# Fused attention and gated MLP: one scaling step of the 64-bit weights on GpSimd instead of ScalarE, with a new order list

## The chip, the cores and the metric

The kernel runs on one core of a Trainium2 chip. A core has five engines that run side by side, each with a queue of its own: TensorE (PE; its weight loads are shown as PEld), VectorE (DVE), ScalarE (ACT), GpSimd (POOL) and SyncE (SP), which here only issues transfers. The metric is the device time of one execution in microseconds, the median of several runs.

## The reference, cut to what matters

```python
# attention, per batch (8) and head (8); seq = 576, head_dim = 64
scores = scale * np.matmul(q, k.transpose(0, 1, 3, 2))
mask = (rel >= 0) & (rel < 128)
scores = np.where(mask, scores + bias[None], -1000000000.0)
attn = softmax(scores)                      # max subtracted, sum + 1e-9
x = matmul(attn, v), heads side by side     # 8 x 576 x 512
# gated MLP on x
h = gelu_tanh(x @ w_in)                     # w_in 512 x 1024
u, v = h[..., :512], h[..., 512:]
v_n = (v - mean) / sqrt(var + 1e-06) * g_ln
v_s = einsum('ts,bsd->btd', w_sg, v_n) + b_sg
out = x + (u * v_s) @ w_out                 # w_out 512 x 512
```

`w_in` and `w_out` come as 64-bit floating point numbers. Each is loaded as pairs of 32-bit words and turned into a high and a low 32-bit part on the chip, and every product with them is three products (high by high, high by low, low by high).

## The kernel before, in words

The work is cut into small named steps. `add` registers a step with its engine, a length and the steps it comes after; the text `ORDER` lists all of them, and they are emitted in exactly that order, so that each engine's queue is the list cut down to that engine's steps. A step waits only for what it reads or overwrites, but nothing on an engine passes the step ahead of it.

There are 32 pairs of heads, four to a batch. For a pair with number n the steps are: `q` and `L` load queries with keys, and values (SP). `a` and `c`, or `*` for both from pair 5 on, are the score products (TensorE). `A B C G` shift and mask the scores and take their minima (VectorE; L305 and L298). `e E f F j` are the exponentials with their sums (ScalarE, L314). `R` inverts the sums (VectorE, L325 and L326; it needs all five exponentials). `r`, `s` (ScalarE for the first four pairs, L332, GpSimd after) and `S` (GpSimd, L337) scale. `z`, `t` and `T` transpose (TensorE, L363 and L350). `P` copies and `X` and `Y` mask the transposes (ScalarE; VectorE, L359). `V` is the product with the values (TensorE, L387). `p` and `x` (ScalarE) and `2` (VectorE, L399) collect it. `h` (ScalarE, L404) and `l` (GpSimd, L221) make its high and low part for the MLP, and `k` copies a tail. In the list the step of the kind `2` for pair 0 reads `20`.

The weights come in twelve blocks k of 128 rows by 512 columns: 0 to 7 for `w_in`, 8 to 11 for `w_out`. Each runs through this chain: `i` loads it (SP, L182) into one of four buffers, which is free again behind `+`. `d` has two ScalarE instructions: L193 scales the low words by 2^-29 in place, from unsigned to signed integers, and L195 takes the absolute value of the high word as a float. `m`, `b` and `o` (VectorE, L197, L199 and L201) clamp, shift and join the bits. `+` (GpSimd, L221) adds the scaled low words, an integer add over all 512 columns. `H` (ScalarE, L206) rounds to the high part, and `-` (VectorE L211 for odd k, GpSimd for even) leaves the low part. `wl`, `wH`, `w-` do the same for the matrix `w_sg`, and `tl`, `tH`, `t-`, `bl`, `bH`, `b-` for its tail and the bias; they share the four buffers. A load that finds none free waits, and the loads behind it on SP's queue wait with it.

The MLP of the first batch begins while the pairs 4 and 5 are in work: `w` followed by two digits and `v0` are the products of the value half (L609 to L611, the first digit is the block of rows, the second the pair), `vg` their gelu (ScalarE, L788; it needs a table load when the last function was an exponential), `nv` and `vn` the normalization, `u` the products of the other half, `uc` their copies (ScalarE, L842), `y` the gate products and `gm` the gating. `W` are idle products on zeros (TensorE, L1141), 51 in twelve steps.

From about 63 us on TensorE does one product behind the other; the later batches use the same steps with fewer products. The part of the list that changes ends in the first fifth of the time.

Of the kernel before, what the change touches and what calls it, by code (L numbers as in the profile page):

```python
# [21 lines left out]
def attention_gmlp(  # L22
# [1125 lines left out]
    for b in range(B):  # L1148
# [14 lines left out]
        r4 S4 w-0 t4 25 X4 nt0b nt0p u010 z4 T4 u011 Y4 nt0c P4 uc02 d11 bH V4 nt0h p4 x4 uc01 ug0 b- tn0 m11 m8 24  # L1163
        b11 o11 b8 y000 y001 *7 +11 gm00 A7 o8 +8 B7 C7 j7 e7 H11 -11 Us0 y020 y021 y030 G7 gm02 Us1 E7 H8 -8 gh00 f7
        h4 gh02 F7 Us2 *6 y010 Us3 R7 A6 B6 C6 s7 t7 S7 T7 y031 E6 gl02 r7 gl00 G6 X7 f6 e6 j6 F6 z7 y011 h5 L7 L6 q8
        q9 Y7 R6 gm03 gm01 P7 V7 gh03 gh01 p7 Uh0 s6 r6 S6 gl01 t6 T6 X6 x7 27 Y6 Oa0 gl03 z6 O00 P6 V6 Us4 oa00 h7
        Uh1 x6 p6 l7 l4 l5 26 Ul0 Ul1 O01 *8 A8 B8 C8 Us5 G8 h6 k5 f8 j8 e8 l6 u100 u101 k6 k7 E8 *9 Us6 F8 oa01 Us7
# [105 lines left out]
```

## Time and profile before

| | us |
|---|---|
| median of 3 runs | 581.13 (581.12 to 581.57) |
| the profiled execution | 581.97 |
| its span, first to last instruction | 580.3 |
| TensorE busy | 563.5 (97%) |
| VectorE busy | 476.9 (82%) |
| ScalarE busy | 381.4 (66%) |
| GpSimd busy | 309.1 (53%) |

The span lies 1.67 us inside the time of its own execution, and that execution 0.84 us above the median. Busy shares over the whole span say little here, since the first 63 us and the rest have different limits; the rows of the next section are read by stretches.

### The profile page before, as it was taken

How to read it: one execution, taken by the hardware profiler on the slowest of the kernel's cores; microseconds unless marked ns; L12 is line 12 of the kernel's file. 1: busy time of each engine (PE TensorE's matmuls, PEld its weight loads, DVE VectorE, ACT ScalarE, POOL GpSimd, SP SyncE). 2: the span in 40 equal slices, each digit the busy share in tenths (PEclk: the TensorE clock that was granted, in tenths of full speed). 3: DMA queues.
4: the chain of work that ended last, by engine and by line, in shares of the span. 5: the costliest groups of instructions: out<-in, count | busy, mean ns of one | idle time of the engine just before them, and what ended most of it. 6: DMA issues, size and time to landing. Idle time of an engine off the chain costs nothing.

```text
span 580.3 us, 14668 instructions
## 1 busy us (share of the span) xinstructions
PE 563.5 (97%) x5495; PEld 514.3 (89%) x5495; DVE 476.9 (82%) x1336; ACT 381.4 (66%) x1066; POOL 309.1 (53%) x365
## 2 busy tenths in 40 slices
PE   6898899999999999999999999999999999999997
PEld 5676799999899799998999998998999989998997
DVE  8998999789989878899787987878897988666646
ACT  7899997375754776568776585746695666833422
POOL 4657645730335643664447753486447653476325
PEclk9979999999999999999999999999999999999999
DMA  8773332080602613454250365135432606012502
GB/s 299 212 224 107 127 102 83 7 272 33 210 37 64 215 37 98 144 180 141 60 184 38 105 236 167 48 101 153 143 121 64 211 4 196 3 32 98 171 1 82
DMA packets 43562, 69.79 MB, mean 120 GB/s; under 512 B 3554, under 2 KB 31202, under 8 KB 43492
## 3 DMA queue, kind: packets, MB, share of 16 engines
q1 hardware_dynamic: 43492, 68.86, 36.8%
q8 instruction: 43, 0.70, 0.5%
q14 instruction: 27, 0.22, 0.1%
HBM read 56.27 MB, written 12.58 MB: 119 GB/s over the span
## 4 chain that ended last, share of the span: by engine, by line
PE 86%; DVE 4%; DMA 3%; ACT 3%; POOL 2%; issue 1%; SPq 0%; DVEq 0%; POOLq 0%
PE ps_m L1061 13%; PE ps_m L609 12%; PE ps_m L907 12%; PE ps_m L611 11%; PE ps_m L610 11%; PE ps_a L350 4%; PE ps_a L281 4%; PE ps_s L387 3%; PE ps_m L387 3%; PE ps_s L281 3%; DMA wst<-w_sgT 2%; DMA qk<-qkT 1%; PE ps_m L943 1%; PE ps_m L942 1%; DVE e L298 1%
## 5 line engine op out<-in xcount | busy, mean ns | idle before, releaser
L337 POOL TENSOR_TENSOR e<-e,rr 128x256 f32<-128x256 f32 (+2 forms) x116 | 80.3, 715 | 95.1 <-DVE rr L326 90.5
L314 ACT ACTIVATE e<-e,stats 128x128 f32<-128x128 f32 (+1 forms) x288 | 110.6, 386 | 19.4 <-DVE stats L298 18.9
L227 POOL TENSOR_TENSOR region<-u,region 128x288 fp32r<-128x288 f32 (+1 forms) x78 | 77.6, 1014 | 44.8 <-ACT region L1008 16.2
L359 DVE TENSOR_TENSOR px<-ps_a,m_both 128x1024 f32<-128x1024 f32 x64 | 77.4, 1215 | 6.2 <-PE ps_a L350 4.9
L609 PE MATMUL ps_m<-ws,region 128*128 128x288 f32 x256 | 78.3, 306 | 0.0
L611 PE MATMUL ps_m<-ws,region 128*128 128x288 f32 x256 | 75.7, 296 | 0.0
L610 PE MATMUL ps_m<-ws,region 128*128 128x288 f32 x256 | 75.6, 295 | 0.0
L732 POOL TENSOR_TENSOR rs<-rs,mhalf 128x1 f32<-128x1 f32 (+1 forms) x40 | 30.6, 766 | 58.3 <-DVE rs L729 54.6
L221 POOL TENSOR_TENSOR xs<-xf,xs 128x288 fp32r<-128x288 f32 (+1 forms) x48 | 51.1, 1086 | 14.5 <-ACT xs L404 14.5
L314 ACT ACTIVATION_READ_ACCUMULATOR e<-e,stats 128x1 f32 x288 | 54.3, 189 | 0.0
L1008 ACT ACTIVATE region<-u 128x576 fp32r<-128x576 f32 x35 | 23.6, 684 | 43.4 <-PE ps_m L610 17.4
L609 PEld LDWEIGHTS ps_m<-ws,region 128*128 128x128 f32 x256 | 48.3, 189 | 1.5 <-issue 1.1
L610 PEld LDWEIGHTS ps_m<-ws,region 128*128 128x128 f32 x256 | 48.2, 188 | 0.1
L611 PEld LDWEIGHTS ps_m<-ws,region 128*128 128x128 f32 x256 | 48.1, 188 | 0.1
L609 PE MATMUL ps_m<-wi,xs 128*128 128x512 f32 x112 | 46.7, 417 | 0.9 <-ACT vg L788 0.9
L1068 DVE TENSOR_TENSOR xf<-ps_m,xf 128x576 f32<-128x576 f32 x48 | 35.7, 750 | 10.9 <-PE ps_m L1061 10.1
L611 PE MATMUL ps_m<-wi,xs 128*128 128x512 f32 x112 | 44.3, 395 | 0.0
L610 PE MATMUL ps_m<-wi,xs 128*128 128x512 f32 x112 | 44.2, 395 | 0.0
L948 DVE TENSOR_TENSOR u<-ps_m,u 128x576 f32<-128x576 f32 x32 | 24.0, 750 | 19.7 <-PE ps_m L943 12.6
L350 PE MATMUL ps_a<-ident,e 128*128 128x128 f32 x256 | 38.0, 276 | 0.2
L298 DVE CUSTOM_DVE_ANT_0 e<-ps_s,bias 128x128 f32<-128x128 f32 (+1 forms) x140 | 34.9, 286 | 2.6
L1061 PE MATMUL ps_m<-region,sum 128*128 128x288 f32 x252 | 36.5, 298 | 0.0
(213 smaller groups left out, 1606.2 us busy)
## 6 DMA issues: line engine op xcount, KB each, us to landing
qk<-qkT SPq DMA_DIRECT2D x32, 576.0 KB, 4.5
sum<-store SPq DMA_DIRECT2D x36, 512.0 KB, 5.0
...
```

The lines of the kernel that those rows point to most:

```text
L221: (engine or nc.gpsimd).tensor_tensor(out[:, cs], a[:, cs], b[:, cs], op)
L227: nc.gpsimd.tensor_tensor(out[:, fs], a[:, fs], b[:, fs], ALU.subtract)
L298: nc.vector.tensor_tensor_reduce(out=dst, in0=src, in1=bs, scale=-1.0 / math.sqrt(D), scalar=3e38, op0=ALU.add, op1=ALU.min, accum_out=acc)
L314: nc.scalar.activation(x, x, AF.Exp, bias=self.nm[0:n, i:i + 1], scale=-1.0, accum_out=self.sm[0:n, i:i + 1])
L337: nc.gpsimd.tensor_tensor(x[:, z:z + step, :], y[:, z:z + step, :], self.rr[0:n, i + z:i + z + min(k, step)].rearrange("p (m o) -> p m o", ...
L350: burst([lambda t=t: nc.tensor.transpose(cv[:, t // 2, t % 2], self.pr[j][:, t, :].rearrange("p (h c) -> p h c", h=2), ident[:, j * R:j * ...
L359: nc.vector.tensor_tensor(xv, cv, mv, ALU.mult)
L609: nc.tensor.matmul(dst, ah, bh, start=(first and i == 0), stop=False)
L610: nc.tensor.matmul(dst, ah, bl, start=False, stop=False)
L611: nc.tensor.matmul(dst, al, bh, start=False, stop=(last and i == n - 1))
L907: nc.tensor.matmul(dst, left(n, g, c)[:, ms], right(n, h, c), start=first and c == 0 and k == 0, stop=c == 1 and k == 2, skip_group_check= ...
L1061: nc.tensor.matmul(dst, p, q, start=first and f == 0 and k == 0, stop=f == 1 and k == 2, skip_group_check=True)
```

## The change

The scaling of the low words leaves the step `d` and becomes a step of its own, `n`, on GpSimd (`third`, twelve times). `d` keeps only the absolute value. `+` now comes after both `o` and `n`. The list is new up to `u101`, the second batch's last product of that kind in the changed part; behind it nothing moves. Only the first lines of the two lists are shown, as far as the text follows them.

```diff
--- before.py
+++ after.py
@@ -182,6 +182,11 @@
         nc.sync.dma_start(w[0:src.shape[0]], src)
         return w
 
+    def third(w):
+
+        w0 = w.bitcast(U32).rearrange("p (n t) -> p n t", t=2)[:, :, 0]
+        nc.gpsimd.tensor_scalar(w0.bitcast(I32), w0, 2.0 ** -29, None, ALU.mult)
+
     def split64(hi, lo, w, f, last):
 
 
@@ -189,8 +194,6 @@
         w1 = w.bitcast(I32).rearrange("p (n t) -> p n t", t=2)[:, :, 1]
         w1f = w.bitcast(F32).rearrange("p (n t) -> p n t", t=2)[:, :, 1]
         fi, ri = f.bitcast(I32), w0.bitcast(I32)
-
-        nc.scalar.activation(ri, w0, AF.Copy, scale=2.0 ** -29)
 
         nc.scalar.activation(f, w1f, AF.Abs)
         yield
@@ -545,11 +548,12 @@
             next(got["steps"])
 
         add(f"i{k}", "SP", 1.55, at - 8.0, load, take=[("g", [f"+{k}"])], lag=2.0)
-        add(f"d{k}", "ACT", 1.13, at, begin, [f"i{k}"], take=take_f)
+        add(f"d{k}", "ACT", 0.57, at, begin, [f"i{k}"], take=take_f)
+        add(f"n{k}", "POOL", 0.65, at, lambda: third(got["w"]), [f"i{k}"])
         add(f"m{k}", "DVE", 0.34, at, go, [f"d{k}"], port=True)
         add(f"b{k}", "DVE", 0.43, at, go, [f"m{k}"], port=True)
         add(f"o{k}", "DVE", 0.61, at, go, [f"b{k}"], port=True)
-        add(f"+{k}", "POOL", 1.26, at, go, [f"o{k}"])
+        add(f"+{k}", "POOL", 1.26, at, go, [f"o{k}", f"n{k}"])
         add(f"H{k}", "ACT", 0.55, at, go, [f"+{k}"])
         if k % 2:
             add(f"-{k}", "DVE", 0.62, at, go, [f"H{k}"], port=True)
@@ -1150,85 +1154,85 @@
 
     HALVED_FROM = "v33"
     ORDER = """
-        q0 i2 d2 W8 W1 a0 c0 i1 A0 B0 m2 b2 o2 C0 e0 d1 E0 j0 f0 +2 G0 m1 F0 q1 a1 c1 b1 R0 A1 o1 B1 C1 wl2 i3 q3 i0
-        L0 H2 wH2 W0 G1 s0 -2 S0 +1 w-2 t0 j1 d3 e1 r0 F1 E1 f1 X0 T0 W7 W2 W3 z0 W6 W11 P0 d0 Y0 m3 V0 b3 R1 o3 m0 b0
-        o0 r1 z1 i5 wl3 p0 s1 +0 a3 A3 B3 W4 t1 W5 W10 c3 X1 C3 G3 wH3 d5 x0 e3 H0 f3 E3 20 S1 +3 w-3 -0 q2 L1 i6 i4
-        L2 i7 h0 H1 F3 j3 P1 d6 T1 a2 Y1 A2 B2 l0 V1 R3 m5 s3 b5 -1 m6 o5 b6 o6 d4 x1 m4 21 +6 S3 t3 W9 X3 p1 r3 d7 h1
-        j2 E2 e2 m7 c2 C2 G2 w00 z3 T3 w20 w30 f2 F2 P3 +5 l1 Y3 b7 R2 b4 o4 o7 s2 S2 +4 +7 L3 q5 V3 x3 23 i9 wl1 p3
-        wH1 d9 r2 H5 q4 L4 i10 gb tl w10 t2 X2 T2 w11 z2 w01 Y2 H3 P2 h3 H7 V2 x2 p2 H4 l3 m9 b9 -3 -5 22 -7 w31 w21
-        *5 A5 B5 h2 H6 e5 l2 w02 w32 v00 E5 vg00 v03 w12 v01 w22 v02 o9 C5 G5 nv00b nv00c -6 -4 +9 nv00p tH d10 k3 H9
-        nv00h vg01 k2 -9 vn00 m10 b10 o10 vg03 f5 +10 u000 u001 nv30b nv30c nv10b nv30p H10 uc00 j5 nv30h F5 vn03 R5
-        nv10c -10 u030 a4 A4 u031 B4 vg02 k0 k1 e4 nv20b s5 r5 S5 nv10p w-1 t- nv20p t5 z5 c4 u020 X5 T5 C4 G4 Y5
-        nv20c j4 uc03 E4 nv10h tt0 f4 P5 F4 nv20h i11 L5 q6 i8 bl q7 wl0 V5 u021 vn01 R4 vn02 tj0 d8 p5 x5 tg0 wH0 s4
...
+        i2 q0 W3 W5 W0 a0 c0 wl2 i1 d2 m2 b2 o2 A0 n2 +2 B0 wH2 C0 H2 G0 j0 e0 d1 f0 E0 F0 m1 b1 o1 q1 R0 i3 s0 a1 A1
+        B1 c1 t0 C1 G1 w-2 -2 n3 n1 S0 i4 i0 L0 q3 +1 n4 n0 T0 X0 Y0 j1 e1 E1 r0 F1 d3 f1 m3 R1 d0 r1 W6 W2 W1 z0 z1
+        b3 m0 b0 o0 o3 a3 A3 B3 s1 P0 V0 d4 p0 +0 wl3 wH3 H0 E3 x0 q2 L1 i6 S1 W11 t1 X1 W10 c3 C3 +3 -0 w-3 i7 q4 gb
+        i5 L2 G3 T1 W9 a2 20 Y1 A2 B2 n6 f3 j3 d6 h0 P1 F3 e3 l0 H1 m6 m4 R3 r3 b6 b4 o6 V1 o4 -1 s3 j2 x1 21 t3 d5 d7
+        e2 H3 p1 k0 +4 S3 +6 n5 X3 m7 m5 w20 c2 C2 G2 z3 T3 w30 W8 W7 E2 h1 l1 P3 f2 F2 i9 L3 q5 i10 d9 Y3 b7 V3 w21
+        R2 o7 b5 o5 m9 s2 t2 S2 n7 +7 +5 x3 23 p3 H6 h3 H4 d10 r2 X2 tl wl1 T2 w00 Y2 w10 z2 P2 V2 H5 k1 x2 l3 p2 w01
+        W4 m10 b9 -3 22 o9 *5 h2 tH wH1 H7 k3 A5 B5 E5 e5 w31 l2 -4 -6 n9 w32 w11 w02 v00 vg00 w12 v01 v03 C5 b10 -5
+        -7 o10 nv00b nv00c nv00p +9 n10 vg01 nv00h H9 G5 vn00 vg03 u000 u001 w22 v02 j5 +10 -9 nv30b nv30c nv10b nv30p
+        uc00 H10 F5 nv30h f5 -10 vn03 R5 nv10c u030 a4 u031 s5 A4 B4 r5 S5 nv10p k2 vg02 nv20b w-1 nv20p t- e4 uc03
+        nv10h E4 t5 X5 z5 c4 C4 G4 u020 T5 tt0 Y5 nv20c f4 j4 F4 P5 nv20h L4 wl0 L5 q7 q6 bl i11 i8 V5 vn01 R4 vn02
...
```

## Rows read from the trace of the kernel before

**Rows 1.** Stretches: start:end, length, busy PE, PEld, DVE, ACT, POOL; clock; DMA.

```profile
10.00:46.70 36.70, 32.15 (x329) 24.89 (x321) 34.81 (x118) 33.88 (x118) 23.15 (x18) 0.91 0.73 231
46.70:63.30 16.60, 14.21 (x131) 11.18 (x130) 13.83 (x43) 14.94 (x36) 11.01 (x9) 1.00 0.41 131
63.30:100.00 36.70, 36.61 (x393) 33.45 (x394) 33.84 (x111) 32.96 (x95) 20.66 (x21) 1.00 0.28 89
```

**Rows 2.** Waits of TensorE, 0 to 70 us: total us, times, longest us.

```profile
PE ps_m L609 <- ACT vg L788: 1.3, 2, 0.9
...
PE ps_m L609 <- ACT u L842: 1.1, 1, 1.1
```

**Rows 3.** Timeline of ScalarE, one step d: start us, length us, instruction.

```profile
33.09 0.67 ACT L193 ACTIVATE wst<-wst 128x512 int32<-128x512 uint32 x1
33.65 0.66 ACT L195 ACTIVATE tmp<-wst 128x512 f32<-128x512 f32 x1
```

**Rows 4.** GpSimd's instructions by form, 0 to 150 us: busy us, mean ns.

```profile
L221 POOL TENSOR_TENSOR tmp<-tmp,wst 128x512 int32<-128x512 int32 x12 | 16.2, 1352 | 25.8 <-DVE tmp L201 17.4 <-ACT e L332 4.3 <-ACT tmp L195 4.1
...
masks.py:199 POOL TENSOR_SCALAR_AFFINE_SELECT ident<-ident 128x128 f32<-128x128 f32 x1 | 0.3, 286 | 0.0
L134 POOL COPY ident<-ident 128x64 f32<-128x64 f32 x1 | 0.2, 236 | 0.1
```

**Rows 5.** Timeline of GpSimd: +3 and the instruction behind it.

```profile
24.43 1.30 POOL L221 TENSOR_TENSOR tmp<-tmp,wst 128x512 int32<-128x512 int32 x1
25.69 1.41 POOL L221 TENSOR_TENSOR ws<-wst,ws 128x576 fp32r<-128x576 f32 x1
```

**Rows 6.** Timeline of VectorE and GpSimd: m7, then S2 and o4.

```profile
36.55 0.74 DVE L197 TENSOR_SCALAR tmp<-tmp 128x512 f32<-128x512 f32 x1
...
40.90 1.04 POOL L337 TENSOR_TENSOR e<-e,rr 128x512 f32<-128x512 f32 x1 [1.05 <-DVE rr L326]
41.04 1.45 DVE L201 SCALAR_TENSOR_TENSOR tmp<-wst,tmp 128x512 int32<-128x512 int32 x1
```

**Rows 7.** Line L201, step o: duration ns min/median/max, first and last start us.

```profile
L201 DVE SCALAR_TENSOR_TENSOR tmp<-wst,tmp x12: 629/692/1445, 8.9 to 88.2; 128x512 int32<-128x512 int32 x12
```

**Rows 8.** Timeline of the opening: set-up's end, a0, d2, e0.

```profile
4.25 1.30 DVE L128 TENSOR_SCALAR bias<-setup 128x448 f32<-128x448 f32 x4 [0.43 <-ACT setup L115]
...
4.66 1.56 PE L281 MATMUL ps_s<-qk 64*64 64x128 f32 x20 [1.06 <-DMA qk<-qkT]
...
6.03 0.67 ACT L193 ACTIVATE wst<-wst 128x512 int32<-128x512 uint32 x1 [1.81 <-DMA wst<-w_in]
...
7.15 0.39 ACT L314 ACTIVATE e<-e,stats 128x128 f32<-128x128 f32 x1
```

**Rows 9.** Timeline of VectorE: m1, b1, R0, o1, B1; then X2 and Y2.

```profile
11.11 0.42 DVE L197 TENSOR_SCALAR tmp<-tmp 128x512 f32<-128x512 f32 x1
11.56 0.43 DVE L199 TENSOR_SCALAR tmp<-tmp 128x512 int32<-128x512 int32 x1
11.92 0.17 DVE L325 TENSOR_SCALAR rr<-stats 128x9 f32<-128x9 f32 x1
...
13.14 1.17 DVE L201 SCALAR_TENSOR_TENSOR tmp<-wst,tmp 128x512 int32<-128x512 int32 x1
14.24 0.28 DVE L305 COPY_PREDICATED ps_m<-sel,ps_m 128x128 f32<-128x128 uint8 x1
...
43.61 2.34 DVE L359 TENSOR_TENSOR px<-ps_a,m_both 128x1024 f32<-128x1024 f32 x2
```

**Rows 10.** Timeline of TensorE and ScalarE: V2, table load, vg00, u030.

```profile
46.67 1.58 PE L387 MATMUL ps_s<-px,vt 64*64 64x128 f32 x36
...
53.30 1.28 ACT L1239 ACT_TABLE_LOAD   x1
...
54.70 0.58 ACT L788 ACTIVATE vg<-ps_m 128x512 f32<-128x512 f32 x1
...
63.34 0.40 PE L609 MATMUL ps_m<-xs,wi 128*128 128x288 f32 x1 [1.11 <-ACT u L842]
```

More of the change, by code (lines that the diff above doesn't have):

```diff
@@ L1163, in attention_gmlp @@
[L1163 to L1167, printed above, removed]
@@ new lines, in attention_gmlp @@
+        p4 uc01 ug0 m8 b8 b- tn0 y020 y021 o8 m11 b11 24 o11 *7 +8 n11 +11 A7 gm02 B7 Us0 j7 H11 H8 E7 -8 C7 f7 e7 G7
+        Us1 -11 F7 y000 y001 gm00 R7 y030 *6 A6 B6 C6 y031 G6 gh00 gh02 e6 f6 j6 r7 s7 S7 gl00 gl02 z7 t7 E6 P7 F6 X7
+        y010 T7 y011 R6 Y7 gm01 L7 q8 L6 q9 gh01 V7 p7 s6 S6 r6 t6 gl01 T6 Us2 gm03 gh03 x7 X6 27 h5 Y6 Oa0 z6 gl03
+        O00 Uh0 oa00 Us3 Ul0 h4 h7 P6 V6 x6 p6 26 Us4 h6 O01 *8 A8 B8 C8 Us5 G8 f8 Uh1 Ul1 j8 e8 l4 l5 l6 l7 u100 u101
+        k6 k7 k5 E8 *9 Us6 F8 oa01 Us7 A9 R8 B9 k4 Uh2 j9 uc10 u130 s8 r8 S8 u131 t8 u110 C9 uc13 E9 e9 f9 T8 tt1 X8
@@ new lines, in attention_gmlp @@
+        D11 D10 q15 L13 tj2 U25 uh27 f13 uh26 e13 ue21 A12 B12 ut24 ul27 ul26 U26 F13 ue25 U23 uh24 E12 ue26 U27 C12
+        ue23 G12 R13 e12 f12 j12 F12 U22 ue27 R12 ul24 U24 ue22 r12 s12 z12 t12 S12 tg2 nt2b nt2p s13 X12 nt2c ue24
+        v22 T12 Y12 v23 vg22 nv22b P12 nt2h tn2 vg23 V12 p12 x12 nv32b nv32c 212 nv22c nv22p nv32p S13 h12 l12 r13 ug2
+        nv22h nv32h ya200 ya210 *14 A14 B14 vn22 ya201 t13 ya211 z13 vn23 y200 y201 X13 gm20 C14 y210 y211 y220 T13
+        gm21 G14 E14 P13 f14 gh21 j14 F14 e14 Y13 gl21 y221 *15 y230 R14 A15 gt21 B15 gm22 C15 r14 s14 S14 y231 gh25
@@ new lines, in attention_gmlp @@
+        f15 gm23 gl25 gt23 gt22 z14 t14 V13 E15 gh23 P14 p13 x13 gh27 O21 gh22 j15 X14 213 lo21 q16 lo22 D13 q17 D12
+        lo20 L14 L15 T14 O25 G15 Y14 gh26 V14 p14 F15 x14 e15 gl23 gl27 gl22 oa21 gl26 O26 oa25 O23 ut35 gt24 214 R15
+        oa26 oa23 *16 A16 B16 C16 O27 s15 S15 r15 z15 t15 h14 k12 gh24 h13 E16 P15 j16 l13 gl24 l14 G16 oa27 X15 k13
+        e16 uh35 F16 f16 O22 T15 Y15 O24 *17 R16 oa22 oa24 A17 B17 V15 s16 r16 S16 x15 p15 215 h15 ul35 l15 C17 f17
+        e17 t16 X16 T16 G17 ut37 Y16 L16 q19 lu32 D21 lu30 D23 L17 q18 lu31 D20 v30 z16 k15 k14 j17 P16 F17 E17 tt3
@@ new lines, in attention_gmlp @@
+        tj3 *18 V16 R17 ut36 tg3 vg30 nt3b nt3c nt3p uh37 x16 ul37 nt3h v31 216 nv03b tn3 U31 uh36 vg31 ue31 U35 A18
+        B18 nv13b ut34 ul36 U36 r17 s17 t17 z17 ue35 uh34 ue36 C18 nv13c U33 ue33 X17 S17 nv03p nv13p ul34 U37 U32
+        ue37 T17 U34 nv13h P17 j18 E18 f18 vn31 ue32 G18 nv03c Y17 nv03h ue34 p16 F18 e18 vn30 v33 D22 R18 *19 vg33
+        V17 x17 ug3 A19 s18 B19 C19 nv33b 217 nv33c v32 t18 ya310 vg32 E19 nv23b nv23c r18 S18 nv33p nv23p j19 ya300
+        ya301 z18 ya311 X18 nv23h nv33h p17 vn32 vn33 e19 h17 G19 h16 P18 F19 l17 k17 f19 lo32 L19 L18 lo31 q20 q21
@@ new lines, in attention_gmlp @@
+        T31 Y31 gm62 y630 y631 gm63 h30 gh65 k29 gh63 gt63 gl65 O61 gt62 O65 gh67 P31 V31 gh66 k28 p31 gh62 x31 oa61
+        gl66 oa65 O66 gl63 gl67 gl62 oa66 231 O63 oa63 gt64 h31 l30 l31 O67 k30 gh64 k31 O62 tt7 gl64 oa67 O64 ut75
+        v71 v70 uh75 ul75 oa64 ut76 ut77 tj7 oa62 ut74 U71 uh77 uh76 tg7 ue71 vg71 nt7b nt7c lu71 D61 lu72 lu70 U75
+        ul77 ul76 ue75 U76 U73 lo70 D63 D62 lo71 D60 lo72 ue76 ue73 nt7p nt7h uh74 ul74 U77 tn7 ue77 vg70 nv17b nv07b
+        nv17p nv07p U72 nv17c nv07c nv17h U74 ue74 nv07h vn71 v72 vg72 vn70 ue72 nv27b nv27c v73 vg73 nv27p ug7 nv27h
@@ L1232, in attention_gmlp @@
+        nv37b nv37p nv37c vn72 nv37h vn73 ya710 ya711 ya700 ya701 y700 y701 y710 gm70 y711 y720 gm71 y721 gh71 gl71
+        y730 y731 gt71 gm72 gm73 O71 gh75 gl75 gh72 gl72 gt72 gh76 gh73 oa71 gt73 gl76 gh77 O75 oa75 gt74 O72 gl73
+        gh74 gl77 gl74 O76 oa76 O73 oa72 oa73 D70 D71 O77 oa77 oa79 O740 O741 oa740 oa741 D73 D720 D721
     """
```

105 lines of the change are left out of this document (41 added, 64 removed).

## The prediction, made blind

> **What bounds the kernel now.** I read the stretches first, then the waits, then the order of single instructions on one engine at a time. TensorE sets the time from 63.3 us on: it is busy 36.61 of 36.70 us up to 100 us, and both lists put the same products there in nearly the same order (behind `u101` they are identical) [rows 1]. So the change can only move the moment at which TensorE becomes dense. Ahead of that it idles 4.55 us from 10 to 46.7 and 2.39 us from there to 63.3 [rows 1]; the waits put the latter on ScalarE, 1.3 us on the gelu of the first value sums (L788) and 1.1 us on the copy of the first u product (L842) [rows 2]. The reader is to see that from 10 to 46.7 us VectorE (34.81 of 36.70 us) is fuller than ScalarE (33.88), and GpSimd has 13.55 us to spare [rows 1].
>
> **What is taken away and added.** Of step `d`, the scaling at L193 goes. Started back to back, an L193 and the L195 behind it are 0.56 us apart [rows 3], so twelve of them free 6.7 us of ScalarE. They come back as twelve steps `n` on GpSimd. The trace shows no single-input multiply on 512 columns of GpSimd. From below: a copy of 64 columns takes 236 ns and a select of 128 takes 286 ns [rows 4], 0.78 ns a column, so 286 + 384 x 0.78 = 0.59 us. From above: the two-input integer add on the same strided words takes 1.35 us [rows 4]. The list's own price is 0.65, and where its prices can be tested they hold: it gives `+` 1.26, and the starts 24.43 and 25.69 are 1.26 apart [rows 5]. The lower end is also nearer in kind (one input), so I take 0.65: 7.8 us in all, at most 16.2. Either fits GpSimd's spare time.
> [...]
>
> What the freed ScalarE time is worth is nothing by itself while VectorE, whose work the change leaves alone, is the fuller. If VectorE were not full, the cover would be ScalarE's own 2.82 us of idle there, and up to the 6.7 us would show. The gain or loss must come from the new order, in four stages.
>
> **Opening, to the start of `B1`.** Before, `q0` lands first and its products start at 4.66; `i2` lands behind it, and L193 starts at 6.03 [rows 8]. VectorE is through its set-up at 4.25 + 1.30 = 5.55 [rows 8]. The new list issues `i2` ahead of `q0`, so the scores start near 6.0 instead, and VectorE fills the hole with `m2 b2 o2` (0.42 + 0.43 + 0.69 [rows 7, 9] and gaps, 1.6 us), to 7.15. That is a gain of about 0.7 us, but it is given back: ScalarE now has `H2` ahead of `j0` and `e0`, and `H2` waits for `+2` (7.15, 0.15 to start and 1.30 [rows 5]: 8.6). Everything behind it on ScalarE waits too: `j0 e0 d1 f0 E0 F0`. Before, these six ran from 7.15 [rows 8] to the start of `R0` at 11.92 [rows 9], 4.77 us; less 0.56 of `d1` they take 4.2. With `H2` to 9.15 `F0` ends at 13.3, and `R0`, which needs it, starts 1.4 us later than before. But `o1`, which occupied VectorE from 13.14 to 14.24 between `A1` and `B1` [rows 9], is by then done. `R0` and `A1` took from 11.92 to 13.14, 1.22 us, so `B1` starts at 13.3 + 1.22 = 14.5 against 14.24: **0.3 us lost**.
>
> **From there to the end of `Y2`.** Before, 14.24 to 43.61 + 2.34 = 45.95 [rows 9], 31.7 us of almost unbroken VectorE. The new list does the same steps and `m9` besides, **+0.45**. VectorE idles 1.89 us there [rows 1], of which two holes, ahead of `C3` and `R3`, make 0.74; the new list fills them (`m6` and `m4` now lie between `B2` and `R3`), **-0.74**. What opposes it is GpSimd. `o4` started 0.14 us behind `S2` and took 1.45 us, where the median `o` takes 0.69 [rows 6, 7]; `m7` took 0.74 [rows 6] where `m1` took 0.42 [rows 9]. These two cost about 1.1 us. By the new list five groups may meet GpSimd: `m6` with `l0` (0.6), `m7` with `S3` (0.35), `m5` with `+6` (1.3), `o7` with `S2` (0.8), `b5 o5 m9` with `n7` and `+7` (0.6), 3.65 us if VectorE comes second in all and nothing if it comes first. I take something under half, 1.6: **+0.5** against before.
> `Y2` then ends at 45.95 + 0.3 + 0.45 - 0.74 + 0.5 = 46.45. Before, TensorE took up `V2` only at 46.67, since products stood ahead of it [rows 10]; in the new list those come behind. `V2` at 46.5: **-0.15** for the first two stages.
>
> **From `V2` to `u030`.** Before, 46.67 to 63.34 = 16.67 us [rows 10], of which 2.4 us are waits, two for the gelu and one for the copy [rows 2]. The new list puts `W4` (0.55) behind `V2`. The wait for the copy goes: `w22` and `v02` stand behind `u001`, 1.45 us that cover the copy. The first for the gelu, 0.9 [rows 2], grows: `w12` still waits for the gelu of `v00`, which comes behind `E5`, `e5` and a table load of 1.28 (to 54.70 [rows 10]). `A5` at 3.9 us behind `V2`, `B5` and the exponentials to 7.2, the table and the gelu to 9.2, against products that are through at 7.9: 1.35. The second is 0.15. So 16.67 - 2.4 + 0.55 + 1.35 + 0.15 = 16.3, say 16.4 with a start: **-0.27**.
>
> **Behind it.** TensorE is dense; `s5` and `t5` follow the last exponential `f5` with some 0.7 us to spare. Nothing taken.
>
> **Moved transfers.** All loads stand on SP's one queue. A load that waits for a buffer holds up those behind it: `i9` now waits for `+4` and has `L3` behind it, about 36 us against 33, while `V3` needs `L3` near 40. The other loads that move (`i4 i0`, `wl3`, later `i8` and `i11`) land before their first readers by more than a microsecond in this working. Taken at nothing; up to 1 us if `L3` is late, since `V3`, `x3`, `23` and `X2` follow one another.
>
> **Sum.** 0.3 + 0.45 - 0.74 + 0.5 - 0.67 (`V2` started 0.72 behind `Y2` and now starts 0.05 behind it) - 0.27 = -0.4 us. The profiled execution took 581.97 (580.3 span and 1.67 around it); less 0.4 it is 581.55. That execution lies 0.84 above the median of 581.13, so the median to expect is 580.7.
>
> **The rivals.** *The order wins* (0.33): GpSimd comes second at every meeting. For it speaks that before, most `m`, `b` and `o` have GpSimd idle beside them; against it that GpSimd gets twelve instructions more. The 1.6 us fall away: 580.7 - 1.6 = 579.1.
> *The shared access decides* (0.20), slower: VectorE comes second in all five, 3.65 us instead of 1.6, 580.7 + 2.05 = 582.8. It decides from about 3.2 us of such waits on. For it speaks the 1.45 us of `o4`, against it that two such meetings in 30 us is all that was paid before. [...]
> *A late `L3`* (0.06): 581.7.
> *The change does not do what it says*: `n` costs 1.35 and the twelve fill GpSimd. Then the meetings get longer, and the time is the second rival's; its chance is in that one.
>
> **How the numbers follow.** My own case has 0.41, its range 579.9 to 581.6. The 0.2% about which a measurement of this kernel can tell from no change is 1.16 us (its three runs lie 0.45 apart): faster is below 579.97, slower above 582.29. Faster: 0.33 and 0.03 of my case. Slower: 0.20 and 0.03 from the rest. Same: 0.41. The range reaches from the first rival to the second, 578.9 to 582.8.
>
> **What would show it.** `n` rows of 0.59 to 0.81 us on GpSimd; `R0` at about 13.3; `B1` at 14.5; `Y2` ending at 46 to 47; `w12` waiting over 1 us for L788 and no wait of `u030` on L842; `u030` near 63. Wrong would be: `R0` before 12.5 (then `H2` held nothing up), rows of `o` and `m` over 1 us in more than three places (second rival), or TensorE gaps behind 65 us.

## The result, and the profile after

The changed kernel took 588.66 us (median of 4 runs, 588.29 to 589.01) against 581.35 (581.12 to 581.60) of the kernel before: a ratio of 1.0125, 95% interval 1.0110 to 1.0141. It is 7.3 us slower; the forecast was 580.7, with 582.8 as its upper end. The profiled execution took 588.72 us, its span is 587.0 (before 580.3), so the trace has 6.7 us to explain. Below, the line numbers of the changed kernel are 3 or 4 higher than those of [rows 1 to 10].

The page's busy times, of the changed kernel:

```profile
PE 563.0 (96%) x5495; PEld 513.6 (87%) x5495; DVE 483.2 (82%) x1336; ACT 375.8 (64%) x1054; POOL 327.2 (56%) x377
```

VectorE has the same 1336 instructions as before and is busy 6.3 us longer (476.9 before); ScalarE is relieved of 5.6 us. Nothing was added on VectorE, so it is held in instructions that it had already. The new line, durations in ns as min/median/max:

```profile
L188 POOL TENSOR_SCALAR wst<-wst x12: 1541/1620/1935, 4.3 to 92.2; 128x512 int32<-128x512 uint32 x12
```

One `n` takes 1.62 us; the working put it at 0.65, between 0.59 and 1.35. The stretches of [rows 1], and the one from `B1` to the end of `Y2`, for the changed kernel; columns as there:

```profile
10.00:46.70 36.70, 27.34 (x300) 20.68 (x301) 33.34 (x113) 30.62 (x117) 29.59 (x22) 0.86 0.67 225
46.70:63.30 16.60, 13.30 (x121) 10.11 (x120) 15.15 (x40) 10.85 (x27) 11.64 (x10) 1.00 0.20 57
63.30:100.00 36.70, 35.01 (x352) 31.32 (x355) 33.52 (x91) 31.89 (x82) 24.53 (x22) 1.00 0.36 113
15.63:50.43 34.80, 26.47 (x270) 19.82 (x269) 32.49 (x97) 27.75 (x99) 27.88 (x21) 0.91 0.56 187
```

The same stretch in the kernel before, and in a run with the new list and no scaling on any engine (below):

```profile
14.24:45.95 31.71, 27.16 (x282) 21.00 (x281) 30.03 (x97) 28.89 (x100) 20.41 (x16) 0.89 0.70 213
```

```profile
14.46:47.33 32.87, 24.77 (x270) 18.95 (x269) 32.04 (x97) 27.82 (x99) 20.53 (x16) 0.94 0.65 212
```

From `B1` to `Y2` it is 34.80 us instead of 31.71. VectorE's busy time rose from 30.03 to 32.49, and its idle time, the rest of the stretch, from 1.68 to 2.31 where the working had it fall by 0.74. Without any scaling the idle time does fall, to 0.83, but the busy time is 32.04 all the same.

Stage by stage, against the terms of the sum (us; starts from the timelines of both kernels):

| stage | before | after | change | predicted |
|---|---|---|---|---|
| to the start of `B1` | 14.24 | 15.63 | +1.39 | +0.3 |
| `B1` to the end of `Y2` | 31.71 | 34.80 | +3.09 | +0.21 |
| to the start of `V2` | 0.72 | 0.14 | -0.58 | -0.67 |
| `V2` to `u030` | 16.67 | 17.05 | +0.38 | -0.27 |
| `u030` to `u101` | 52.81 | 54.52 | +1.71 | 0 |
| `u101` to the end | 464.15 | 464.86 | +0.71 | 0 |
| sum | 580.3 | 587.0 | +6.7 | -0.4 |

**Opening.** Timelines of the changed kernel, VectorE: the set-up of the bias, `m2`, `o2`, `R0` and `B1`.

```profile
4.24 2.21 DVE L128 TENSOR_SCALAR bias<-setup 128x448 f32<-128x448 f32 x4 [0.43 <-ACT setup L115]
6.38 0.41 DVE L200 TENSOR_SCALAR tmp<-tmp 128x512 f32<-128x512 f32 x1
...
7.28 0.69 DVE L204 SCALAR_TENSOR_TENSOR tmp<-wst,tmp 128x512 int32<-128x512 int32 x1
...
14.09 0.37 DVE L328 TENSOR_SCALAR rr<-stats 128x9 f32<-128x9 f32 x1 [0.28 <-ACT e L317]
...
15.63 0.30 DVE L308 COPY_PREDICATED ps_m<-sel,ps_m 128x128 f32<-128x128 uint8 x1
```

GpSimd: `n2`, `+2`, then `n3` and `n1` as one row, and `S0`.

```profile
4.28 1.94 POOL L188 TENSOR_SCALAR wst<-wst 128x512 int32<-128x512 uint32 x1 [0.93 <-DMA wst<-w_in]
...
8.13 1.28 POOL L224 TENSOR_TENSOR tmp<-tmp,wst 128x512 int32<-128x512 int32 x1 [1.92 <-DVE tmp L204]
...
12.12 3.23 POOL L188 TENSOR_SCALAR wst<-wst 128x512 int32<-128x512 uint32 x2
15.43 1.04 POOL L340 TENSOR_TENSOR e<-e,rr 128x512 f32<-128x512 f32 x1
```

The reader is to see the first meeting of the new step. `n2` runs from 4.28 to 6.22, and the four bias instructions beside it take 2.21 us where they took 1.30 [rows 8]. Neither is at its usual length: `n2` has 1.94 against a median of 1.62. `m2`, and with it `+2`, `H2` and the exponentials behind `H2`, are 0.9 late by that. Then `n3` and `n1` hold GpSimd until 15.35.

**The meetings.** VectorE's `m7` and `m5` as one row, then `o7`, `b5` and `o5`; and GpSimd's `+6`, `S2` and `n7` beside them:

```profile
38.48 2.11 DVE L200 TENSOR_SCALAR tmp<-tmp 128x512 f32<-128x512 f32 x2
...
44.03 0.63 DVE L204 SCALAR_TENSOR_TENSOR tmp<-wst,tmp 128x512 int32<-128x512 int32 x1
44.58 1.27 DVE L202 TENSOR_SCALAR tmp<-tmp 128x512 int32<-128x512 int32 x1
45.88 1.05 DVE L204 SCALAR_TENSOR_TENSOR tmp<-wst,tmp 128x512 int32<-128x512 int32 x1
```

```profile
38.83 1.47 POOL L224 TENSOR_TENSOR tmp<-tmp,wst 128x512 int32<-128x512 int32 x1
...
44.28 1.27 POOL L340 TENSOR_TENSOR e<-e,rr 128x512 f32<-128x512 f32 x1 [0.79 <-DVE rr L329]
45.64 1.65 POOL L188 TENSOR_SCALAR wst<-wst 128x512 int32<-128x512 uint32 x1
```

`m7` and `m5` take 2.11 us, where two of `m1`'s length would take 0.84; `b5` takes 1.27 where `b1` took 0.43 [rows 9], `o5` 1.05 where the median was 0.69 [rows 7]. Each has an instruction of GpSimd beside it: `S3` and `+6` beside `m7` and `m5`, `S2` beside `b5`, `n7` beside `o5`. Only one of these is a new step. The run with the new list and no scaling, which has no `n` at all, holds the same steps of VectorE; `m7` and `m5`, `b5`, `o5`, then GpSimd's `S3`, `+6`, `S2` and `+7`:

```profile
35.26 2.12 DVE L200 TENSOR_SCALAR tmp<-tmp 128x512 f32<-128x512 f32 x2
...
41.15 1.26 DVE L202 TENSOR_SCALAR tmp<-tmp 128x512 int32<-128x512 int32 x1
42.45 1.68 DVE L204 SCALAR_TENSOR_TENSOR tmp<-wst,tmp 128x512 int32<-128x512 int32 x1
```

```profile
34.62 1.04 POOL L340 TENSOR_TENSOR e<-e,rr 128x512 f32<-128x512 f32 x1
35.62 1.48 POOL L224 TENSOR_TENSOR tmp<-tmp,wst 128x512 f32<-128x512 f32 x1
...
40.86 1.27 POOL L340 TENSOR_TENSOR e<-e,rr 128x512 f32<-128x512 f32 x1 [1.85 <-DVE rr L329]
42.09 1.49 POOL L224 TENSOR_TENSOR tmp<-tmp,wst 128x512 f32<-128x512 f32 x1
```

Of the 2.46 us by which VectorE's busy time rose in this stretch, 2.01 are there without `n` (32.04 - 30.03); 0.45 of them are `m9`. With `n` it is 0.45 more in the changed kernel. In the run with `r4` first (below), whose list is the same up to `n8`, it is 1.48 more, so one profiled run fixes this only to about 1 us:

```profile
15.77:50.12 34.35, 24.93 (x270) 18.54 (x269) 33.52 (x97) 27.86 (x99) 27.83 (x21) 0.95 0.58 193
```

**Behind it.** The two waits of [rows 2] and the start of `u030` [rows 10] in the changed kernel; then the wait that is new, with GpSimd's `n8` and `r4`:

```profile
PE ps_m L613 <- ACT vg L792: 1.2, 1, 1.2
...
PE ps_m L613 <- ACT u L846: 0.3, 1, 0.3
```

```profile
67.62 0.40 PE L613 MATMUL ps_m<-xs,wi 128*128 128x288 f32 x1 [0.29 <-ACT u L846]
...
84.74 0.33 PE L366 MATMUL ps_a<-ident,e 128*128 128x128 f32 x1 [1.20 <-POOL e L340]
```

```profile
82.65 1.56 POOL L188 TENSOR_SCALAR wst<-wst 128x512 int32<-128x512 uint32 x1 [0.64 <-DMA vt<-v_in]
84.29 0.40 POOL L340 TENSOR_TENSOR e<-e,rr 128x128 f32<-128x128 f32 x1
```

TensorE, which the working called dense from 63 us on, waits 1.20 us for `r4`, which stands behind `n8` on GpSimd; ahead of `n8` GpSimd itself had waited 0.64 us for a transfer. Behind `u101`, where the two lists are the same, another 0.71 us are lost; TensorE has a wait of 0.5 us for VectorE there (L989) that the kernel before has not.

### The profile page after: what moved, and what is told of

Read it like the earlier page. It is cut to its first block, busy times and chain, and to the rows that moved or that the text cites. A ratio compares the mean times of both kernels' runs of the same rounds, so it can differ in the third digit from the quotient of the medians.

```text
span 587.0 us, 14666 instructions
## 1 busy us (share of the span) xinstructions
PE 563.0 (96%) x5495; PEld 513.6 (87%) x5495; DVE 483.2 (82%) x1336; ACT 375.8 (64%) x1054; POOL 327.2 (56%) x377
## 4 chain that ended last, share of the span: by engine, by line
PE 85%; DVE 5%; ACT 3%; POOL 2%; DMA 2%; issue 2%; SPq 0%; DVEq 0%; ACTq 0%; POOLq 0%
PE ps_m L1065 13%; PE ps_m L613 12%; PE ps_m L911 11%; PE ps_m L615 11%; PE ps_m L614 11%; PE ps_a L353 5%; PE ps_m L390 4%; PE ps_a L284 3%; PE ps_s L390 3%; PE ps_s L284 3%; DMA wst<-w_in 1%; PE ps_m L947 1%; PE ps_m L946 1%; DVE px L362 1%; PE ps_m L802 1%
## 5 line engine op out<-in xcount | busy, mean ns | idle before, releaser
L224 POOL TENSOR_TENSOR xs<-xf,xs 128x288 fp32r<-128x288 f32 (+1 forms) x48 | 49.7, 1056 | 15.7 <-ACT xs L407 15.6
L353 PE MATMUL ps_a<-ident,e 128*128 128x128 f32 x256 | 39.4, 280 | 3.5 <-POOL wst L188 2.2
L353 PEld LDWEIGHTS ps_a<-ident,e 128*128 128x128 f32 x256 | 30.7, 142 | 7.6 <-issue 3.7
```

The lines of the kernel that those rows point to most:

```text
L224: (engine or nc.gpsimd).tensor_tensor(out[:, cs], a[:, cs], b[:, cs], op)
L353: burst([lambda t=t: nc.tensor.transpose(cv[:, t // 2, t % 2], self.pr[j][:, t, :].rearrange("p (h c) -> p h c", h=2), ident[:, j * R:j * ...
```

## The experiments

**The scaling and the list, apart.** Three kernels cross them: the new list with the scaling on ScalarE, the new list with the scaling nowhere, the old list with `n` on GpSimd ahead of each `+`. A fourth has the old list and the scaling nowhere.

The new list with the scaling on ScalarE:

```diff
+        nc.scalar.activation(ri, w0, AF.Copy, scale=2.0 ** -29)
         nc.scalar.activation(f, w1f, AF.Abs)
...
-        add(f"n{k}", "POOL", 0.65, at, lambda: third(got["w"]), [f"i{k}"])
+        add(f"n{k}", "POOL", 0.65, at, lambda: None, [f"i{k}"])
```

> The new list with the scaling put back into step d on ScalarE; the steps n stay in the list but issue nothing. If the loss is the price of n (1.62 us measured against the 0.65 that I took), it is gone here: 580.5 to 583 us, VectorE busy near the 476.9 us of before. If the new order itself is what loses, this stays at 587 us or above.

The new list with the scaling nowhere; `n` is empty as above, and the add takes the high words as floats:

```diff
-        by_halves(ALU.add, fi, fi, ri)
+        by_halves(ALU.add, f, f, w1f)
```

> The new list with the scaling left out altogether: n issues nothing, d keeps only the absolute value, and the add behind them (step +) adds the high words as floats instead of the low ones, so that the weights are other numbers. This is the new list with n at a price of nothing. Price theory: 579.5 to 581.5 us, at or below the scaling on ScalarE. Order theory: 587 us or above.

The old list with `n` directly ahead of each `+` (the first of twelve places):

```diff
-        q0 i2 d2 W8 W1 a0 c0 i1 A0 B0 m2 b2 o2 C0 e0 d1 E0 j0 f0 +2 G0 m1
+        q0 i2 d2 W8 W1 a0 c0 i1 A0 B0 m2 b2 o2 C0 e0 d1 E0 j0 f0 n2 +2 G0 m1
```

> The list of before with each n put directly in front of its + on GpSimd's queue, so that only the engine of the scaling changes. Price theory: each + comes up to 1.7 us later and VectorE's steps are held by a busier GpSimd, 584 to 589 us. Order theory: 581 to 582.5 us, the old list being the good one.

The old list with the scaling nowhere, by the same two edits:

> The old list, with the scaling of the low words on no engine (the integer add of the low words is replaced by an add of the high words as floats, so this part of the weights is left out). It shows what the time freed on ScalarE is worth under the old list, with the order unchanged. The prediction's step (nothing by itself, since VectorE is the fuller engine): 581 to 581.5 us. The rival, that the old order was built around ScalarE's length: up to 577.6, by the 3.7 us that the same removal gave under the new list (588.76 to 585.08).

Measured, as the median, the ratio to the kernel before as it ran beside it, and its interval:

| | scaling nowhere | on ScalarE | `n` on GpSimd |
|---|---|---|---|
| old list | 581.51, 0.9995 (0.9987 to 1.0004) | the kernel before | 588.93, 1.0136 (1.0121 to 1.0151) |
| new list | 585.08, 1.0071 (1.0043 to 1.0099) | 588.76, 1.0135 (1.0109 to 1.0161) | the changed kernel, 1.0125 (1.0110 to 1.0141) |

Read along the rows: under the old list the scaling on ScalarE costs nothing, and on GpSimd 7.4 us (588.93 - 581.51). Under the new list it costs 3.7 us on ScalarE (588.76 - 585.08) and 3.6 on GpSimd (588.66 - 585.08). Read down: the new list costs 4.1 us with no scaling at all (0.0071 of 581) and 7.6 with it on ScalarE. So the change has two losses; each alone is as large as the whole, and they don't add up; how the 7.3 us divide between them can't be said. The run of the new list without scaling scatters from 583.7 to 588.4, and its profiled run is the fastest.

**The price of `n`.** The old list with `n` on 176 columns, and the new list with the same:

```diff
-        nc.gpsimd.tensor_scalar(w0.bitcast(I32), w0, 2.0 ** -29, None, ALU.mult)
+        nc.gpsimd.tensor_scalar(w0.bitcast(I32)[:, 0:176], w0[:, 0:176], 2.0 ** -29, None, ALU.mult)
```

> The old list with n directly ahead of each +, over 176 of the 512 columns (0.79 us each, near the 0.65 that the prediction took; the add is of the high words as floats, so the scaling of the other columns and the add of the low words are left out). If the price of n is the step that failed, a price of 0.79 costs the old list little: 581 to 582.5 us. If any twelve more GpSimd instructions ahead of the adds cost it, whatever their length: near the 588.9 of the full n. In proportion to the length (0.79 of 1.62) it would be 585.

> The new list with n on GpSimd over 176 of its 512 columns, which should bring n to about the 0.65 us of my sum (the low words of the other columns are not scaled, and the add takes the high words as floats, so that the weights are other numbers). This is the case that the prediction described. Price theory: 580 to 582.5 us, between no scaling and the full change and nearer to the former. Order theory: 587 us or above. By the sum of the prediction: 580.7.

The old list: 583.98, ratio 1.0041 (1.0029 to 1.0053). The new list: 587.43, ratio 1.0113 (1.0091 to 1.0135), with runs from 584.59 to 588.57; its twelve `n` took 792 ns each. This is the case that the prediction described, and it lost 6.6 us (0.0113 of 581) where 0.4 were to be gained. So a cheap `n` does not save the new list. GpSimd's row of `n` in the old list (busy us and mean ns behind the bar):

```profile
L188 POOL TENSOR_SCALAR wst<-wst 128x176 int32<-128x176 uint32 x12 | 9.1, 760 | 3.9 <-DMA wst<-w_in 2.9
```

The busy times of the old list's three runs, in the order `n` nowhere, 176 columns, 512 columns:

```profile
PE 561.7 (97%) x5495; PEld 512.6 (88%) x5495; DVE 477.7 (82%) x1336; ACT 375.5 (65%) x1054; POOL 308.6 (53%) x365
```

```profile
PE 564.0 (97%) x5495; PEld 514.3 (88%) x5495; DVE 479.2 (82%) x1336; ACT 375.4 (64%) x1054; POOL 317.6 (54%) x377
```

```profile
PE 565.7 (96%) x5495; PEld 514.6 (88%) x5495; DVE 484.7 (83%) x1336; ACT 376.0 (64%) x1054; POOL 328.3 (56%) x377
```

VectorE's busy time, with the same instructions and the same list, goes up against the kernel before (476.9) by 0.8, 2.3 and 7.8 us, and the time by -0.3, 2.4 and 7.9 us (the ratios times 581). Under the old list the time lost is as large as what VectorE is held. In the profiled run with 512 columns the loss lies in the same two stages as the holding: 3.46 us from `B1` to the end of `Y2` (35.17 us, VectorE busy 34.14 for 30.03) and 3.97 from the start of `V2` to `u030` (20.64 us, 17.84 for 13.90), less 0.77 between them. In the second of these ScalarE also waits 3.1 us for GpSimd's adds (0.2 before), so that GpSimd's own lateness has a part in it isn't excluded.

What makes `n` so long was asked of four forms in one kernel, three instructions each on 512 columns. Two forms work on a spare tile, one reads the high words, and nothing uses the results (the add takes the high words as floats):

```diff
-        nc.gpsimd.tensor_scalar(w0.bitcast(I32), w0, 2.0 ** -29, None, ALU.mult)
+        out, src = [(w0.bitcast(I32), w0), (f0, w1f), (u.bitcast(I32), u), (dummy, dummy)][k % 4]
+        nc.gpsimd.tensor_scalar(out, src, 2.0 ** -29, None, ALU.mult)
```

> The new list with n in four forms over 512 columns, three of each, whose results nobody uses (the add behind them takes the high words as floats, so that the weights are other numbers): k = 0, 4, 8 as in the change (unsigned in, signed out, every second word); k = 1, 5, 9 floats in and out, every second word; k = 2, 6, 10 unsigned in, signed out, contiguous; k = 3, 7, 11 floats in and out, contiguous. If the conversions make n dear: 1.6 us for the unsigned forms, 0.6 to 0.8 for both float forms. If the stride makes it dear: 1.6 for both strided forms, 0.6 to 0.8 for the contiguous ones. If one input on GpSimd simply costs that much: all near 1.6.

GpSimd's rows by form (`wst` strided, `dummy` contiguous):

```profile
L195 POOL TENSOR_SCALAR dummy<-dummy 128x512 int32<-128x512 uint32 x3 | 4.9, 1619 | 0.3
L195 POOL TENSOR_SCALAR wst<-wst 128x512 f32<-128x512 f32 x3 | 4.8, 1596 | 0.2
L195 POOL TENSOR_SCALAR wst<-wst 128x512 int32<-128x512 uint32 x3 | 4.7, 1583 | 0.6 <-DMA wst<-w_out 0.5
L195 POOL TENSOR_SCALAR dummy<-dummy 128x512 f32<-128x512 f32 x3 | 4.7, 1554 | 0.2
```

All four lie between 1554 and 1619 ns. So here neither the conversion nor the stride makes the price; in all four forms the multiply with one input took longer on GpSimd than the integer add with two (1352 ns [rows 4]).

**Where the list loses.** Scaling on ScalarE, with the list put together from both: the old one up to `Y0`, or up to `V2`, and the new order behind it; and the new one up to `Y0` and the old order behind it.

The first line of the new list in the kernel with the old one up to `V2`, where it goes over to the new order:

```diff
-        i2 q0 W3 W5 W0 a0 c0 wl2 i1 d2 m2 b2 o2 A0 n2 +2 B0 wH2 C0 H2 G0 j0
+        q0 i2 d2 W8 W1 a0 c0 i1 A0 B0 m2 b2 o2 C0 e0 d1 E0 j0 f0 +2 G0 m1
...
-        R2 o7 b5 o5 m9 s2 t2 S2 n7 +7 +5 x3 23 p3 H6 h3 H4 d10 r2 X2 tl wl1 T2 w00 Y2 w10 z2 P2 V2 H5 k1 x2
+        wH1 d9 r2 H5 q4 L4 i10 gb tl w10 t2 X2 T2 w11 z2 w01 Y2 H3 P2 h3 H7 V2 k0 w21 m9 H6
```

> Scaling on ScalarE in step d. The old list up to Y0 (the first 18.8 us of before), behind it the new list's order for everything that is left. The new list with the same scaling took 588.8. If the new list loses in its opening (H2 ahead of the exponentials, all idle products at the front, V0 behind z1), this falls to 581 to 583 us. If it loses later, it stays at 586 us or above.

> The old list up to V2 and the rest in the new order, the scaling on ScalarE as before. The prediction put the stretch behind V2 at a gain of 0.27 us: 581 us. If the new list loses behind V2 too: 583 or more. With the old list up to Y0 it was 585.83, so at 581 the loss behind Y0 would lie all between Y0 and V2.

> The counterpart of the old list up to Y0: the new list up to Y0 and the old order behind it, the scaling on ScalarE as before (wl3 moved behind +0, since its buffer is free only then). If the opening of the new list costs 2.9 us for itself and the loss behind Y0 is the other part's alone: about 584. If the two parts of the list lose only where they meet other steps they were not made for: 586 or more. If the opening's delay is absorbed by idle time further on, as the prediction took it: 581 to 582.

Measured: old up to `Y0` 585.83 (1.0081, 1.0058 to 1.0104), old up to `V2` 584.53 (1.0048, 1.0036 to 1.0060), new up to `Y0` 587.35 (1.0105, 1.0088 to 1.0122). The loss is not in one place: each part of the new list loses when joined to the rest of the old, and the parts (6.1 us for the opening, 4.6 behind it) sum to more than the 7.6 of the whole. The new order behind `V2` alone costs 2.8 us (0.0048 of 581), where the prediction had a gain of 0.27. The opening alone costs more than the 2.9 us by which the old list up to `Y0` improves on the whole new list (588.76 - 585.83).

**The opening's `V0`.** In the changed kernel `V0` starts at 23.58 us (18.88 before), since `P0` waits behind `s1` on ScalarE, and VectorE's `X1` then waits for `t1`, which stands behind `V0` (VectorE's waits in the stretch from `B1` to `Y2`; total us, times, longest):

```profile
DVE px L362 <- PE ps_a L353: 1.3, 1, 1.3
```

Six kernels change this: `V0` early behind the idle products `W6 W2 W1` (scaling on ScalarE); `z0 P0 V0` ahead of them (with `n`, and on ScalarE); the same with the idle products further back (both); and with them left out (with `n`). One more kernel moves `W0` only.

`V0` early, behind the idle products, and then `V0` first:

```diff
-        F1 d3 f1 m3 R1 d0 r1 W6 W2 W1 z0 z1 b3 m0 b0 o0 o3 a3 A3 B3 s1 P0 V0 d4
+        F1 d3 f1 W1 W2 W6 z0 P0 m3 R1 d0 r1 V0 z1 b3 m0 b0 o0 o3 a3 A3 B3 s1 d4
```

```diff
-        F1 d3 f1 m3 R1 d0 r1 W6 W2 W1 z0 z1 b3 m0 b0 o0 o3 a3 A3 B3 s1 P0 V0 d4
+        F1 d3 f1 m3 R1 z0 P0 d0 r1 V0 W6 W2 W1 z1 b3 m0 b0 o0 o3 a3 A3 B3 s1 d4
```

The latter with the idle products further back, and with them left out:

```diff
-        W11 t1 X1 W10 c3
+        W11 t1 W6 W2 W1 X1 W10 c3
```

```diff
-            for i in range(n):
+            for i in range(0 if k in (1, 2, 6) else n):
```

And `W0` alone, in the list with the scaling on ScalarE:

```diff
-        i2 q0 W3 W5 W0 a0 c0 wl2
+        i2 q0 W3 W5 a0 c0 wl2
...
-        B1 c1 t0
+        B1 c1 W0 t0
```

> The new list with scaling on ScalarE in step d, and one thing put back as in the old list: z0, P0 and V0 stand ahead of r1, z1 and a3 instead of behind them. Theory of the waiting V0: V0 starts near 20 us instead of 23.6, the wait of X1 (1.3 to 2.2 us of VectorE) goes, and the time falls by 2 to 4 us, to 585 to 587. Clock theory (the cold stretch of TensorE behind the early idle products sets the loss): no change, 588 to 589.

> The new list with scaling on ScalarE in step d, and one thing put back as in the old list: the twelve idle products W0 stand behind c1 instead of ahead of a0. Clock theory: the granted clock from 10 to 20 us goes back from 0.83 to 1.0, V0 and the transposes run at full speed, and the time falls by 2 to 4 us, to 585 to 587. Theory of the waiting V0: V0 still waits for r1 and the second half of P0, no change, 588 to 589.

> The changed kernel with one place of its list set back: z0, P0 and V0 (the first pair's second transpose, its copy and its product with the values) go ahead of the steps of pair 1 and of three groups of idle products, as in the old list. V0 started 4.7 us later than before in the changed kernel and X1 3.4 us later. If the place of V0 in the queues makes the loss of the opening: V0 at 20 to 21 us, X1 1.5 to 2.5 us earlier, the time 586.2 to 587.2. If VectorE, held by GpSimd, is what is late: V0 earlier, but the time 588 to 589.

> The new list with the scaling on ScalarE as before and with the same place of z0, P0 and V0 set back. If their place in the queues makes the 2.9 us that the opening of this list costs: about 586 instead of 588.76. If the opening is late because ScalarE does H2 ahead of the exponentials and the scalings ahead of P0, whatever the place of V0: 588 to 589.

> As V0 first, but the three groups of idle products W6 W2 W1 go behind t1 and X1's reads are no longer behind them on TensorE (with V0 first alone, they took 2.4 us between V0 and z1, and X1 stayed late). If TensorE's queue in the opening makes the loss of the opening: z1 at 22 to 23.3, X1 at 25 to 26 (27.07 in the changed kernel), the time 586.5 to 587.5. If VectorE, held by GpSimd, is what is late: X1 earlier, but Y2 still ends near 50 and the time stays at 588 to 589.

> The same two moves with the scaling on ScalarE. If TensorE's queue in the opening makes the loss of this list without n: X1 at 25 to 26 (27.89 in the run of this list with the scaling on ScalarE), the time 585.5 to 586.8 instead of 588.4 to 588.8. If it only moves to the next late thing: 588 or more.

> As V0 first (n on GpSimd), with the products of the three idle groups W6 W2 W1 left out, so that neither z1 nor c3 stands behind them. If TensorE's queue in the opening makes the loss there: X1 at 25 to 26, R3 at 31.5 to 32.5 (33.87 in the changed kernel), Y2 ending at 48 to 49.2, the time 586 to 587.4. If VectorE's own length decides: X1 earlier, R3 and the end of Y2 as in the changed kernel (33.9, 50.4), the time 588 to 589.

| | `V0` | `X1` | `R3` | time, ratio and interval |
|---|---|---|---|---|
| changed kernel | 23.58 | 27.07 | 33.87 | 588.66 |
| `V0` early, on ScalarE | 22.10 | 27.68 | 34.48 | 589.00, 1.0133 (1.0115 to 1.0151) |
| `W0` late, on ScalarE | 23.09 | 27.26 | 34.07 | 588.56, 1.0134 (1.0107 to 1.0161) |
| `V0` first, with `n` | 19.69 | 28.27 | 35.07 | 590.29, 1.0154 (1.0135 to 1.0172) |
| `V0` first, on ScalarE | 19.18 | 28.34 | 35.14 | 588.37, 1.0131 (1.0111 to 1.0150) |
| idle behind, with `n` | 19.48 | 25.89 | 34.74 | 590.10, 1.0152 (1.0137 to 1.0168) |
| idle behind, on ScalarE | 19.19 | 25.93 | 34.79 | 588.92, 1.0132 (1.0115 to 1.0149) |
| idle left out, with `n` | 19.67 | 26.59 | 33.48 | 588.69, 1.0123 (1.0101 to 1.0146) |

None is faster, beyond its scatter, than the kernel that it was made from (588.66 with `n`, 588.76 with the scaling on ScalarE), so the lateness of `V0` alone isn't shown to be the cause. But none is a clean test either: each mended one wait and made another (`z1` behind the idle products at 25.35, then `c3` behind them), and where `V0` started some 4 us earlier it took 3.3 us. The stretch of `V0` in the changed kernel, with `r4` first (below), and with the idle products left out; the third column from the end is the granted clock:

```profile
23.58:26.07 2.49, 2.49 (x47) 2.39 (x41) 1.83 (x13) 0.11 (x1) 2.49 (x3) 0.66 0.10 21
```

```profile
22.96:24.61 1.65, 1.65 (x51) 1.55 (x43) 1.62 (x8) 0.89 (x3) 1.16 (x1) 1.00 0.03 8
```

```profile
19.67:23.02 3.35, 3.35 (x42) 2.39 (x41) 3.25 (x8) 2.92 (x12) 1.45 (x1) 0.50 0.91 315
```

The same products took 1.65 us where the granted clock was 1.00, 2.49 where it was 0.66, and 3.35 where it was 0.50. The run with `r4` first has the list of the changed kernel up to `n8`; at `V0` it differs by the clock (1.00 for 0.66) and by 0.6 us in the start. There `X1` starts at 25.61 without a wait, VectorE's idle time in the stretch is 0.83 us instead of 2.31, but `m6` and `m4` beside `l0` take 1.92 us instead of 0.76, and `Y2` ends at 50.12, only 0.31 earlier. The wait went, and a meeting took most of its place.

**`n8` and `r4`.** The changed kernel with these two exchanged on GpSimd:

```diff
-        ... 25 X4 nt0b S4 n8 r4 w-0
+        ... 25 X4 nt0b S4 r4 n8 w-0
```

> The changed kernel with n8 behind r4 on GpSimd instead of ahead of it. In the changed kernel TensorE waits 1.20 us for r4's result ahead of z4, behind 84 us, where it otherwise has no gap. If that wait comes from the 1.6 us of n8 alone: 1.2 us less, 587.5. If the wait only moves to the next thing late (r4 behind S4, or m8 and b8 behind n8): no change, 588.7.

The median is 588.50, ratio 1.0128 (1.0111 to 1.0144). TensorE's `z4` in this run:

```profile
83.07 0.27 PE L366 MATMUL ps_a<-ident,e 128*128 128x128 f32 x1
```

The wait of 1.20 us is gone, and `u030` to `u101` takes 53.12 us instead of 54.52: in its place the 1.4 us are shown. In the median they aren't: the runs lie between 587.45 and 588.80, as far apart as the gain is large.

## Why the prediction was wrong, step by step

**The price of `n`** is the first term of the sum that failed: "From above: the two-input integer add on the same strided words takes 1.35 us", "The lower end is also nearer in kind (one input), so I take 0.65". The measured 1.62 us lies outside both ends. The upper bound rested on the belief that one input can't cost more than two, and the lower on a copy and a select of at most 128 columns; neither operation is a multiply. The list's price of 0.65 was no evidence: it had been right for `+` and was wrong for `n`. Under the old list this price is worth 5.0 us (588.93 - 583.98), but under the new one 1.2 (588.66 - 587.43, within the scatter). With `n` at 0.79 the forecast still fails by 6.7 us, so the larger failure is in what the working said of the new order. No run shows the 0.81 us that the prediction looked for as the upper end of the rows of `n` on 512 columns: in the changed kernel the twelve lie between 1.54 and 1.94 us, and among the four forms contiguous words (1554 and 1619 ns) took as long as strided ones (1583 and 1596).

**The meetings** are the second, and the order's own: "I take something under half, 1.6". VectorE's busy time from `B1` to `Y2` rose by 2.46 us; less 0.45 for `m9` that is 2.0 net, where 0.5 was predicted (1.6 less the 1.1 already paid before). Taken as the prediction took them that makes 3.1 of the 3.65, which was the author's estimate. Three of the five groups that it named were held: `m7` and `m5` (2.11 us for both), and `b5 o5`, these more than thought. `m6` with `l0` (0.76 for `m6` and `m4`) and `o7` with `S2` (0.63) were not, since `S2` met `b5` instead; `R1`, which the working did not name, was (its first row, beside GpSimd's `n4` and `n0`, took 0.60 us, that of `R0` 0.17 [rows 9]). The second rival, that VectorE comes second in nearly all, fits the busy time of this stretch. Its 582.8 was too low, since it kept the price of `n` at 0.65 and the other terms as they were. The run without scaling shows this step apart from the first: it has no `n`, and VectorE is busy 32.04 us in this stretch, 1.56 more than before without `m9`, where the working allowed 0.5.

**The holes**, -0.74, were +0.63 (the 1.89 us of idle time that the working took from [rows 1] belong to a longer stretch; in this one they are 1.68). The new list does fill them, idle time falls by 0.85 us where there is no scaling; with `n` a wait of 1.3 us for the transposes behind the late `V0` came instead.

**The opening's** working came out right with the `n` that it assumed: with a cheap `n` of 0.79 us `R0` starts at 13.40 and `B1` at 14.74, without scaling at 13.12 and 14.46; predicted were 13.3 and 14.5. With the real `n` they are 14.09 and 15.63, since `n2` meets the bias set-up, which the working didn't consider.

**`V2` to `u030`**: 17.05 us, 16.4 predicted. The wait for the gelu grew to 1.17 as thought (1.35), that for the copy shrank to 0.29 where none was left in the working.

**"Behind it. TensorE is dense"**, nothing taken: 1.71 us were lost up to `u101`, 1.2 of them at `z4`. The working followed `s5` and `t5` and not `n8`, which stands ahead of `r4` on GpSimd. The new order behind `V2` costs 2.8 us even with the scaling on ScalarE, where there is no `n8`; which step loses there stays open.

**Right** were that ScalarE's freed time is worth nothing by itself (581.51 under the old list), and that `V2` starts right behind `Y2` (0.14 us). A slip without effect: the first rival stands at 579.1, and the range begins at 578.9.

**What stays open.** Why the new list loses 4.1 us where no engine does the scaling: in its profiled run, 1.7 us longer in span than before, `X3` is 1.3 us ahead of before and `Y2` ends 1.4 late, and the held `m5`, `b5` and `o5` lie between; the rest is in runs that have no profile. The granted clock of these is on record: without scaling the mean over the run was 0.988 where the time was 588.42 us, and 0.991 to 0.997 in the other four (583.72 to 585.55); with 176 columns 0.988 in the two runs of 588.55 and 588.57, and 0.994 and 0.996 at 584.59 and 586.31. That fits a clock that sets part of the scatter, but it isn't shown: the run at 0.997 took 585.55. Why the scaling on ScalarE costs 3.7 us under the new list and nothing under the old was narrowed to the stretch ahead of `X1` (27.89 with it, 23.85 without), but no move in the opening gave it back. Of these 4.0 us, 2.4 are there at the start of `V0` (23.57 and 21.21); `V0` then took 2.83 us at a clock of 0.50 and 1.53 at 1.00. The clock is not all of it: two runs with `W0` late had a mean of 0.997 and 0.994, as the kernel before has (0.993 to 0.999), and took 587.99 and 588.15. What in GpSimd's instructions holds VectorE's is not shown: the rows show that VectorE's are longer beside them (`b5` 1.27 us beside `S2`, `b1` 0.43 [rows 9]). That it is an access which the two share, as the second rival has it, was the author's assumption; no run here took GpSimd's access to memory away and left its time.
